# An FNet layer with a GEGLU block: wider loads of the DFT weights, another order of the first tiles, an earlier gate/up tile, down weights two steps ahead, and a plain tail

## The chip, the cores and the metric

The kernel runs on one core of a Trainium2 chip. Its engines work in parallel, each through its own queue in order: PE (TensorE, matmuls), PEld (its weight loads), DVE (VectorE), ACT (ScalarE), POOL (GpSimd) and SP (SyncE, which only issues DMAs here). The metric is the time on the device in microseconds, the median of several executions; lower is better. One further execution is recorded by the hardware profiler; its times of single instructions are used throughout.

## The reference

One sequence of 2048 tokens with 448 features, 1792 hidden features, all in float32.

```python
def mixing(x, seq_re, seq_im, hid_re, hid_im):
    a = jnp.einsum("bsd,ed->bse", x, hid_re)
    b = jnp.einsum("bsd,ed->bse", x, hid_im)
    return jnp.einsum("ts,bse->bte", seq_re, a) - jnp.einsum("ts,bse->bte", seq_im, b)

def geglu(x, w_gate, w_up, w_down):
    g = jnp.einsum("bsd,df->bsf", x, w_gate)
    u = jnp.einsum("bsd,df->bsf", x, w_up)
    return jnp.einsum("bsf,fd->bsd", gelu(g) * u, w_down)

h = x + mixing(layernorm(x), seq_re, seq_im, hid_re, hid_im)
out = h + geglu(layernorm(h), w_gate, w_up, w_down)
```

## The kernel before

Every float32 operand is split into two float16 parts, a high one (rounded, made on ACT by `hi_part`, line 100) and a low one (the remainder, made on DVE by `lo_part`, lines 104 and 106). A product is three float16 matmuls: high by high, high by low, low by high. Many products are done in Strassen form, which saves an eighth of the matmuls and pays with sums of blocks on DVE and POOL.

**Feature DFT.** x comes as 16 tiles of 128 tokens (`x_load`, line 307). Each is normalised, split, transposed by PE or by DMA (`x_turn`) and multiplied with the hidden DFT matrix: `feature_mm(i)`, slot "F", 22 matmuls of 448 columns in 11 steps of 2 (line 404). `feature_out` copies the result from PSUM (the tile `ab`) into the operands `b` of the next stage; for tiles of Strassen units it goes first into a float32 tile of the buffer ring "w" (two buffers).

**Sequence DFT.** 8 passes p over 256 output tokens each, with 8 units u of 256 input tokens in each pass: slot "U", `seq_mm(p, u)`, line 491. Units 5, 6 and 7 are Strassen units: 42 matmuls of 224 columns. The other five have 24 matmuls of 448. A unit's weights are loaded by SP into `wr` (`seq_load`, line 458, four buffers), summed on DVE if it is a Strassen unit (`seq_sums`, lines 463 to 465) and split into `ws` (`seq_split`, three buffers): high parts on ACT, low parts on DVE. `seq_out` (line 518 and the lines around it) ends a pass and adds the residual into `hx`. Pass 0 runs between the F slots; in passes 1 to 7, the FFN's layer norm and transposes for the passes that are done run beside it.

**Gate/up weights.** Between the units, 14 tiles of the gate and up weights are prepared (class `Weights`): loaded (line 538), summed on DVE (`gu_s`, lines 543 to 546), split on ACT and DVE into `gu_w` (also in the ring "w"; 4 sums and 4 splits on DVE for each tile), and stored by SP to DRAM (`w_dram`, line 571). The FFN loads them again as `gw` (line 928).

**Order.** The order of both DFTs is a plan: `plan(slot, rank, work)` puts a piece of work into a slot of the list `slots`; a slot's pieces are issued in the order of their ranks, and then its matmuls. What comes ahead of slot 3 is written out by hand.

**FFN.** 4 blocks of tokens by 14 tiles, in 56 steps t. `GateUp(t)` (line 848) has the matmuls into `pX`, `pY`, `pZ`, whose results are combined by DVE (line 858, `u`, `hh`, `c`), ACT and POOL. From step 14 on each step also has 21 down matmuls (line 791, `acc_d <- wd, dn_w`) for hidden tiles done earlier; `dn_w` is split on ACT and DVE. The down weights `wd` come in 7 tiles: `down_load(n)` (line 193), `down_sums(n)` on POOL (lines 198 to 201, `wd_s`), then splits in `down_prep(k)`, k = 0 to 13, two for each tile, on ACT and DVE.

**Tail.** After step 55, down products of the last hidden block remain for four output tiles of 128 tokens. One of the four is made plain (`last_mm`, line 1011: 84 matmuls of 224 columns) into the PSUM bank `last_tr`; two are made as a Strassen pair (`last_sums`, `last_split`, `last_pair_mm`: 147 matmuls, and sums `last_v`, `last_s`, `last_a` on DVE, POOL and ACT); the last is made plain into two banks, X and Y. `h_last` are the split hidden tiles, `hr` the tiles with the residual that go out (line 1023).

Of the kernel before, what the change touches and what calls it, by code (L numbers as in the profile page):

```python
# [8 lines left out]
F16 = mybir.dt.float16  # L9
# [4 lines left out]
P = 128  # L14
# [18 lines left out]
def kernel(  # L33
# [157 lines left out]
    def down_load(n):  # L191
        wd32[n] = fops.tile([P, 4, HD], F32, tag="xn" if n % 2 else "tt", name=f"wd32_{n}")
        nc.sync.dma_start(wd32[n].rearrange("p (k c) d -> p k (c d)", k=2), w_down[n])
# [100 lines left out]
    first = ExitStack()  # L294
    p1 = first.enter_context(tc.tile_pool(name="p1", bufs=1, side="right"))
# [85 lines left out]
    def wh_high(k):  # L381
        hi_part(wh_hi[:, k, :], wh_raw[k // 2][:, k % 2, :], D_SC)
# [12 lines left out]
    def feature_mm(i, parts=range(2), tag="B"):  # L395
        if 0 in parts:
            feat[i] = [ps_dft.tile([P, 512], F32, tag=tag, name=f"ab{i}_{r}") for r in range(2)]
        steps = [[], [(k, wh_lo, k) for k in range(4)]]
        for k in range(4):
            steps[0] += [(k, wh_hi, k)] + ([(4 + k, wh_hi, k)] if k < 3 else [])  # L400
        for part in parts:
            for n, (kx, w, kw) in enumerate(steps[part]):
                for r in range(2):
                    PE.matmul(  # L404
                        feat[i][r][:, :D],
                        xT[i][:, kx, :],
                        w[:, kw, r * D : (r + 1) * D],
                        start=part == 0 and n == 0,
                        stop=part == 1 and n == 3,
                    )  # L410
# [44 lines left out]
    def seq_load(p, u):  # L455
        wr[p, u] = dft.tile([P, 4, 2 * P], F32, tag="wr", bufs=4, name=f"wr{p}_{u}")
        for g in range(2):
            nc.sync.dma_start(wr[p, u][:, 2 - 2 * g : 4 - 2 * g, :], w_seq[p * N_UNIT + u, :, g::2, :])

    def seq_sums(p, u):  # L460
        r = wr[p, u]
        s = wsum[p, u] = dft.tile([P, 4, 2 * P], F32, tag="wsum", bufs=2, name=f"wsum{p}_{u}")
        V.tensor_add(s[:, 0:2], r[:, 0:1].to_broadcast([P, 2, 2 * P]), r[:, 1:3])  # L463
        V.tensor_add(s[:, 2], s[:, 0], r[:, 2])
# [14 lines left out]
    PRODUCTS = [(1, 0, 2, 0), (2, 2, 0, 1), (6, 1, 0, 0), (0, 6, 1, 1), (3, 3, 2, 1), (5, 5, 3, 0), (4, 4, 3, 1)]  # L479

    def seq_mm(p, u, first, last):
# [4 lines left out]
        for cc in range(2):  # L486
# [11 lines left out]
            else:  # L498
                for k, a0 in ((0, 2), (1, 0)):
# [165 lines left out]
    for k in range(1, 4):  # L665
        wh_load(k)
# [615 lines left out]
```

## Time and profile before

| | us |
|---|---|
| median of 3 runs | 746.25 (745.68 to 746.96) |
| profiled execution | 745.24 |
| its span in the profile | 743.4 |
| start, up to the first sequence unit | 0 to 31.39 |
| feature DFT and pass 0, to the end of pass 0 | 31.39 to 121.45 |
| passes 1 to 4 and a part of 5 | 121.45 to 284.81 |
| rest of the sequence DFT | 284.81 to 371.63 |
| FFN | 371.63 to 704.84 |
| tail | 704.84 to 743.4 |

A row of the timeline or of the chain reads: start, duration, engine, line of the kernel, operation, output <- inputs, partitions x elements and type, number of instructions; in brackets the engine's idle time ahead of it and what ended it. A row of the waits reads: who waited for whom, us in all, number, the longest.

In the page's division of the span into 40 slices, the busy share of PE in tenths, and its clock, are:

```profile
PE   7999999998989999999999989999999999999987
PEclk9999999999999999999999999999999999999999
```

### The profile page before, as it was taken

To read this page: it belongs to the slowest core of one execution; us is meant where nothing else is said; L and a number is where in the kernel's file an instruction comes from. 1 tells how busy PE (TensorE), PEld (TensorE's weight loads), DVE (VectorE), ACT (ScalarE), POOL (GpSimd) and SP (SyncE) were. 2 spreads that over 40 slices of the span, in tenths; PEclk is the share of its full clock that TensorE was granted. 3 is DMA by queue.
4 is the path that set the end of the run, shared out by engine and by line. 5 is a ranking of instruction groups with operands and counts; after the bars stand their busy time and mean duration, and the time that the engine had idled before them with its cause. 6 is when DMAs were issued, how large, how long until landed. Compare 5 with 4: busy or idle time off the path is not lost.

```text
span 743.4 us, 14813 instructions
## 1 busy us (share of the span) xinstructions
PE 716.3 (96%) x5779; PEld 559.1 (75%) x5779; DVE 599.0 (81%) x1165; ACT 329.4 (44%) x611; POOL 292.8 (39%) x316
## 2 busy tenths in 40 slices
PE   7999999998989999999999989999999999999987
PEld 4455557765656666677688868999999999999987
DVE  5677777898989899989447789788787877989795
ACT  5566553537363634444134444345444434444421
POOL 3033121010101020101047986577676766768460
PEclk9999999999999999999999999999999999999999
DMA  9154444788979789786167744656639475555311
GB/s 313 55 126 102 99 119 156 229 233 270 249 255 242 261 227 348 237 303 229 50 207 265 256 173 167 186 182 178 188 128 254 170 213 216 203 187 210 129 38 38
DMA packets 97927, 142.92 MB, mean 192 GB/s; under 512 B 42305, under 2 KB 81345, under 8 KB 97857
## 3 DMA queue, kind: packets, MB, share of 16 engines
q1 hardware_dynamic: 97856, 141.97, 60.9%
q8 instruction: 45, 0.74, 0.4%
q14 instruction: 26, 0.20, 0.1%
HBM read 112.46 MB, written 20.19 MB: 178 GB/s over the span
## 4 chain that ended last, share of the span: by engine, by line
PE 63%; DVE 21%; ACT 5%; DMA 4%; issue 3%; POOL 2%; SPq 1%; ACTq 0%; DVEq 0%; POOLq 0%
PE acc L491 18%; PE pY L848 12%; PE acc_d L791 11%; PE pX L848 8%; PE pZ L848 8%; PE ab L404 6%; DVE ws L106 5%; DVE gu_w L106 2%; DVE xs L104 1%; DVE wsum L463 1%; DMA x<-in_x_dram 1%; DMA gw<-w_dram 1%; DVE dn_w L104 1%; ACT ws L100 1%; DVE last_v L1032 1%
## 5 line engine op out<-in xcount | busy, mean ns | idle before, releaser
L491 PE MATMUL acc<-b,ws 128*128 128x448 f16 (+1 forms) x1968 | 282.7, 305 | 7.6 <-DVE ws L106 6.8
L491 PEld LDWEIGHTS <-ws 128*128 128x128 f16 x1968 | 188.8, 98 | 100.8 <-DVE ws L106 13.1
L848 PEld LDWEIGHTS <-gw 128*128 128x128 f16 x2067 | 202.3, 98 | 30.2 <-issue 6.5
L848 PE MATMUL pY<-hops,gw 128*128 128x256 f16 x901 | 123.2, 273 | 5.5 <-DVE u L858 5.2
L525 POOL TENSOR_TENSOR hx<-hx,e 128x448 f32<-128x448 f32 x16 | 25.2, 1594 | 253.3 <-DVE e L522 158.6
L791 PE MATMUL acc_d<-wd,dn_w 128*128 128x224 f16 x882 | 105.4, 259 | 0.0
L106 DVE SCALAR_TENSOR_TENSOR ws<-wr,ws 128x1024 f16<-128x1024 f32 (+1 forms) x64 | 76.7, 1199 | 15.0 <-ACT ws L100 14.8
L791 PEld LDWEIGHTS <-dn_w 128*128 128x128 f16 x882 | 85.2, 98 | 3.0
L100 ACT ACTIVATE ws<-wr 128x1024 f16<-128x1024 f32 (+1 forms) x64 | 61.6, 969 | 50.1 <-PE acc L491 25.2
L848 PE MATMUL pX<-hops,gw 128*128 128x256 f16 x583 | 81.3, 273 | 1.7 <-DMA gw<-w_dram 1.7
L848 PE MATMUL pZ<-hops,gw 128*128 128x256 f16 x583 | 79.7, 274 | 0.0
L858 DVE SCALAR_TENSOR_TENSOR u<-pY,u 128x256 f32<-128x256 f32 x112 | 47.0, 420 | 36.6 <-PE pY L848 18.2
L886 ACT ACTIVATE u<-pX 128x256 f32<-128x256 f32 x56 | 21.4, 382 | 90.4 <-PE pX L848 84.9
L404 PEld LDWEIGHTS <-xT 128*128 128x128 f16 x352 | 34.4, 99 | 34.3 <-issue 2.3
L915 POOL TENSOR_TENSOR hh<-hh,g 128x256 f32<-128x256 f32 x42 | 35.9, 855 | 57.8 <-DVE hh L858 57.8
L104 DVE TENSOR_TENSOR dn_w<-dn_s,dn_w 128x640 f16<-128x640 f32 x42 | 52.7, 1254 | 1.6 <-ACT dn_w L100 1.4
L899 ACT ACTIVATE g<-pX 128x256 f32<-128x256 f32 x56 | 21.3, 380 | 70.0 <-PE pX L848 66.5
L404 PE MATMUL ab<-wh_hi,xT 128*128 128x448 f16 x224 | 47.0, 360 | 1.1 <-DVE b L106 0.7
L100 ACT ACTIVATE ws<-wsum 128x1024 f16<-128x1024 f32 x24 | 25.3, 1054 | 50.9 <-DVE wsum L465 50.9
L941 POOL TENSOR_TENSOR dn_s<-hh 128x256 f32<-128x256 f32 x42 | 43.5, 1036 | 0.0
L924 POOL TENSOR_TENSOR hh<-hh,c 128x256 f32<-128x256 f32 x42 | 36.8, 877 | 16.3 <-ACT c L922 16.3
L942 POOL TENSOR_TENSOR dn_s<-hh 128x256 f32<-128x256 f32 x42 | 43.1, 1026 | 0.0
(134 smaller groups left out, 956.8 us busy)
## 6 DMA issues: line engine op xcount, KB each, us to landing
gw<-w_dram SPq DMA_DIRECT2D x53, 896.0 KB, 5.0
wr<-in_w_seq_dram SPq DMA_DIRECT2D x128, 256.0 KB, 4.9
w_dram<-gu_w SPq DMA_DIRECT2D x14, 896.0 KB, 4.8
gu_raw<-in_w_gu_dram SPq DMA_DIRECT2D x28, 384.0 KB, 4.7
wd<-in_w_down_dram SPq DMA_DIRECT2D x14, 448.0 KB, 4.9
hx<-in_x_dram SPq DMA_DIRECT2D x8, 448.0 KB, 5.8
h_dram<-hx SPq DMA_DIRECT2D x8, 448.0 KB, 5.2
hr<-h_dram SPq DMA_DIRECT2D x8, 448.0 KB, 5.4
```

The lines of the kernel that those rows point to most:

```text
L100: A.activation(dst, src, AF.Copy, scale=scale)
L104: V.tensor_sub(dst, src, hi)
L106: V.scalar_tensor_tensor(dst, src, scale, hi, op0=ALU.mult, op1=ALU.subtract)
L404: PE.matmul(feat[i][r][:, :D], xT[i][:, kx, :], w[:, kw, r * D : (r + 1) * D], start=part == 0 and n == 0, stop=part == 1 and n == 3,)
L491: PE.matmul(banks[k][:, cols], lhs, rhs, start=k not in begun, stop=stop, skip_group_check=True)
L791: PE.matmul(acc[k // 2][:, k % 2 * HD : (k % 2 + 1) * HD], a_of(la, a), b_of(lb, b), start=first and m == 0 and k % 2 == 0, stop=last and ...
L848: PE.matmul(ps, w[:, wl, wa + ws, :], ops[:, m + ms, :], start=first and n == 0, stop=last and n == len(terms) - 1, skip_group_check=True,)
L858: V.scalar_tensor_tensor(dst, ps, SC, other, op0=ALU.mult, op1=ALU.add)
L915: G.tensor_mul(c21, c21, self.g1)
L924: G.tensor_mul(c22, c22, self.c12)
L941: G.tensor_add(s[:, 0:2], t[:, 0:2], t[:, 2:4])
L942: G.tensor_sub(s[:, 2:4], t[:, 1:4:2], t[:, 0:4:2])
```

## The change

W's unit comes in one DMA, with rows of 4 KB for each partition, where two DMAs brought two blocks each. The blocks stand in another order, so the sums, the splits and the table of products name others; the split of a Strassen unit's own blocks falls into two pieces, of 256 and 512 elements, where it was one of 768.

```diff
     def seq_load(p, u):
...
-        for g in range(2):
-            nc.sync.dma_start(wr[p, u][:, 2 - 2 * g : 4 - 2 * g, :], w_seq[p * N_UNIT + u, :, g::2, :])
+        nc.sync.dma_start(wr[p, u], w_seq[p * N_UNIT + u])
...
-        V.tensor_add(s[:, 0:2], r[:, 0:1].to_broadcast([P, 2, 2 * P]), r[:, 1:3])
-        V.tensor_add(s[:, 2], s[:, 0], r[:, 2])
-        V.tensor_add(s[:, 3], s[:, 2], r[:, 3])
+        V.tensor_add(s[:, 0:2], r[:, 1:2].to_broadcast([P, 2, 2 * P]), r[:, 0:4:3])
+        V.tensor_add(s[:, 2], s[:, 1], r[:, 0])
+        V.tensor_add(s[:, 3], s[:, 2], r[:, 2])
...
-        parts = [(slice(0, 3), r[:, 1:4]), (slice(3, 7), wsum.pop((p, u)))] if is_s(u) else [(slice(0, 4), r)]
+        parts = [(slice(0, 1), r[:, 0:1]), (slice(1, 3), r[:, 2:4]), (slice(3, 7), wsum.pop((p, u)))] if is_s(u) else [(slice(0, 4), r)]
```

The first of the 14 gate/up tiles is prepared inside the feature DFT, and the other 13 are spread over the passes; a tile's load and its store each come one slot later. `p2`, the pool of their raw tiles, is there from the start. x is loaded, normalised and transposed two slots earlier than before.

```diff
-            plan(n - 8, 8, lambda u=i // 2: x_load(u))
+                plan(n - 10, 8, lambda u=i // 2: x_load(u))
...
-        plan(n - 2, 3, lambda p=p, u=u: seq_split(p, u))
+        plan(n - 2 if g else -3, 3, lambda p=p, u=u: seq_split(p, u))
...
-            plan(g, 9, lambda p=p, u=u: seq_load(p, u))
+            plan((-6, -5, 1, 2)[g], 9, lambda p=p, u=u: seq_load(p, u))
...
-    n0 = p1_end + 4
+    pairs = [where["F", 2 * u] for u in ORDER if is_s(u)]
+    early_f = [s + 4 for s in pairs[1:2]]
+    n0 = p1_end + 3
...
-    at_f = [n0 + k * (len(slots) - 3 - n0) // NF for k in range(NF)]
-    plan(n0 - 3, 9, lambda: gu.update({order[0]: Weights(order[0])}))
+    late_f = NF - len(early_f)
+    at_f = early_f + [n0 + k * (len(slots) - 5 - n0) // late_f for k in range(late_f)]
+    plan(0, 9, lambda: gu.update({order[0]: Weights(order[0])}))
...
-            plan(n + 1, 9, lambda f=order[k + 1]: gu.update({f: Weights(f)}))
-        plan(n + 2, 7, lambda f=f: gu[f].split(False), lambda f=f: gu[f].store())
+            plan(n + 2, 9, lambda f=order[k + 1]: gu.update({f: Weights(f)}))
+        plan(n + 2, 7, lambda f=f: gu[f].split(False))
+        plan(n + 3, 10, lambda f=f: gu[f].store())
```

In the feature DFT, DVE's queue has these rows before, around the Strassen unit 6 of pass 0 (`ws_6`) and the feature tiles 14 and 15 (`b_14`, `b_15`; the numbers at the ends of names are the program's own):

```order
L463 TENSOR_TENSOR wsum_6_962<-wr_6_410 128x512
L464 TENSOR_TENSOR wsum_6_962<-wsum_6_962,wr_6_410 128x256
L465 TENSOR_TENSOR wsum_6_962<-wsum_6_962,wr_6_410 128x256
L106 SCALAR_TENSOR_TENSOR ws_6_990<-wr_6_410,ws_6_990 128x768
L106 SCALAR_TENSOR_TENSOR ws_6_990<-wsum_6_962,ws_6_990 128x1024
L104 TENSOR_TENSOR xs_996<-x_780,xs_996 128x64
L104 TENSOR_TENSOR xs_996<-x_780,xs_996 128x384
```

And these rows now, at the same place of the same queue:

```order
L466 TENSOR_TENSOR wsum_6_985<-wr_6_446 128x512
L467 TENSOR_TENSOR wsum_6_985<-wsum_6_985,wr_6_446 128x256
L468 TENSOR_TENSOR wsum_6_985<-wsum_6_985,wr_6_446 128x256
L106 SCALAR_TENSOR_TENSOR gu_w_989<-gu_raw_419,gu_w_989 128x512
L106 SCALAR_TENSOR_TENSOR gu_w_989<-gu_raw_419,gu_w_989 128x256
L106 SCALAR_TENSOR_TENSOR ws_6_1019<-wr_6_446,ws_6_1019 128x256
L106 SCALAR_TENSOR_TENSOR ws_6_1019<-wr_6_446,ws_6_1019 128x512
L106 SCALAR_TENSOR_TENSOR ws_6_1019<-wsum_6_985,ws_6_1019 128x1024
L106 SCALAR_TENSOR_TENSOR gu_w_989<-gu_s_945,gu_w_989 128x512 x2
L104 TENSOR_TENSOR b_1093<-b_14_1059,b_1093 128x1568
```

The four splits of the early gate/up tile stand between the sums and behind the splits of unit 6, the 768 is a 256 and a 512, and the split of the last x tiles (`xs`) stands further ahead. On ACT the copy into `b_15` now waits for the DMA that stores `gu_w_989`, since both use the same buffer of the ring.

Of the start, written out by hand, this is the core. The loads of x for tiles 0 and 1 stand ahead of the four loads of the hidden matrix, `feature_mm` is cut in parts of its 11 steps, and the high part of the matrix's last block is made on GpSimd.

```diff
-    wh_load(0)
     x_load(0, (slice(1, 2),))
-    for k in range(1, 4):
+    for k in range(4):
         wh_load(k)
     x_load(1)
+    x_load(ORDER[2])
...
+    wh_high(3, G)
...
-    wh_high(3)
...
-    feature_mm(0, (0,))
+    feature_mm(0, range(6))
+    x_stats(2)
     x_turn_pe(1, 0, 4)
     x_turn_pe(1, 4, 7)
+    feature_mm(0, range(6, 7))
```

The down weights are prepared two steps earlier, and their first load and sums lie within the sequence DFT.

```diff
+    plan(len(slots) - 14, 9, lambda: down_load(0))
+    plan(len(slots) - 8, 9, lambda: down_sums(0))
...
-    down_load(0)
     down_load(1)
...
-            if t == 2:
-                down_sums(0)
-            if t > 2:
-                down_prep(t - 3)
+            if t > 0:
+                down_prep(t - 1)
...
-        if t - 3 <= 2 * NC:
-            down_prep(t - 3)
+        if t == 2 * NC:
+            down_prep(t - 1)
```

DVE's queue in step 15 of the FFN (the number behind `u_` is the step) has these rows before:

```order
L858 SCALAR_TENSOR_TENSOR u_15_5102<-pY_5087,u_15_5100 128x256
L106 SCALAR_TENSOR_TENSOR wd<-wd_6_4925,wd 128x448
L104 TENSOR_TENSOR dn_w_5120<-hh_4106,dn_w_5120 128x256
L104 TENSOR_TENSOR dn_w_5120<-dn_s_5050,dn_w_5120 128x640
L858 SCALAR_TENSOR_TENSOR u_15_5146<-pY_5087,u_15_5100 128x256
L858 SCALAR_TENSOR_TENSOR hh_4999<-pZ_5108,u_15_5146 128x256
```

And these now:

```order
L882 SCALAR_TENSOR_TENSOR u_15_5097<-pY_5082,u_15_5095 128x256
L104 TENSOR_TENSOR dn_w_5112<-hh_4101,dn_w_5112 128x256
L104 TENSOR_TENSOR dn_w_5112<-dn_s_5045,dn_w_5112 128x640
L882 SCALAR_TENSOR_TENSOR u_15_5138<-pY_5082,u_15_5095 128x256
L882 SCALAR_TENSOR_TENSOR hh_4998<-pZ_5103,u_15_5138 128x256
```

The split of `wd` is gone from there, and likewise the one of 128x1120 in step 16; the last two now stand in steps 13 and 14, where those of the tile before stood.

The tail makes all four tiles plain. `last_sums`, `last_split` and `last_pair_mm` go.

```diff
-    last_mm(1, 0, banks[:1])
-    for n in range(2):
+    for n, (j, g) in enumerate(((0, 0), (0, 1), (1, 0))):
+        last_mm(j, g, banks[n : n + 1])
         do(N_GU + 1 + n, 3)
...
-        last_pair_mm(n)
...
+        last_out(j, g, banks[n], 0, 2)
+    last_mm(1, 1, banks[3:])
+    for c in range(2):
+        last_out(1, 1, banks[3 + c], c, 1)
```

More of the change, by code (lines that the diff above doesn't have):

```diff
@@ L393, with feature_mm @@
     feat = {}
-    def feature_mm(i, parts=range(2), tag="B"):
-        if 0 in parts:
+    def feature_mm(i, part=range(11), tag="B"):
+        if 0 in part:
             feat[i] = [ps_dft.tile([P, 512], F32, tag=tag, name=f"ab{i}_{r}") for r in range(2)]
[L398 to L410, printed above, removed]
+        steps = [(k, wh_hi, n) for k, n in ((0, 0), (1, 1), (4, 0), (5, 1), (2, 2), (6, 2), (3, 3))]
+        steps += [(k, wh_lo, k) for k in range(4)]
+        for n in part:
+            kx, w, kw = steps[n]
+            for r in range(2):
+                PE.matmul(
+                    feat[i][r][:, :D],
+                    xT[i][:, kx, :],
+                    w[:, kw, r * D : (r + 1) * D],
+                    start=n == 0,
+                    stop=n == 10,
+                )
     HD = D // 2
```

111 lines of the change are left out of this document (43 added, 68 removed).

## The prediction

> **What bounds the kernel now.** I read the page first, then the span cut into its stages, then in each stage the waits of the engine that sets its pace. The page's own lines:
>
> ```profile
> span 743.4 us, 14813 instructions
> PE 716.3 (96%) x5779; PEld 559.1 (75%) x5779; DVE 599.0 (81%) x1165; ACT 329.4 (44%) x611; POOL 292.8 (39%) x316
> PE 63%; DVE 21%; ACT 5%; DMA 4%; issue 3%; POOL 2%; SPq 1%; ACTq 0%; DVEq 0%; POOLq 0%
> ```
>
> TensorE (PE) is busy for 716 of 743 us, so a change that leaves the matmuls alone can win only what PE waits, and what a lowered clock costs after a wait. The chain of work that ended last nevertheless runs through VectorE (DVE) for 21% of the span. The stages tell where (columns: start and end, length, busy us of PE, PEld, DVE, ACT, POOL, each with its count, then clock, DMA share, GB/s):
>
> ```profile
> 8.72:31.39 22.67, 20.21 (x112) 10.02 (x111) 12.85 (x35) 12.67 (x23) 4.32 (x2) 0.93 0.51 170
> 31.39:121.45 90.06, 89.21 (x533) 51.64 (x532) 66.16 (x127) 50.54 (x78) 20.16 (x18) 1.00 0.47 119
> 121.45:284.81 163.36, 155.96 (x1099) 104.51 (x1097) 148.94 (x284) 77.61 (x118) 16.27 (x10) 1.00 0.82 243
> 284.81:371.63 86.82, 86.82 (x604) 58.52 (x605) 71.00 (x119) 34.66 (x50) 6.69 (x4) 1.00 0.67 226
> 371.63:461.46 89.83, 83.11 (x745) 73.17 (x744) 65.09 (x126) 37.86 (x82) 63.37 (x67) 0.98 0.61 213
> 704.84:743.40 38.56, 32.68 (x317) 30.70 (x315) 29.15 (x57) 7.45 (x12) 14.51 (x17) 0.96 0.10 37
> ```
>
> PE waits 2.5 us in the start (first row), 0.9 in the feature DFT, 7.4 in the first half of the sequence DFT, nothing in its second half, 6.7 in the first 90 us of the FFN, and some 3 before the last store in the tail; the 243 us of FFN between the last two rows are full. These are the only places where this change can find time, and the terms below take them one by one.
>
> **The tail: -3.4.** The last seven units of a Strassen pair (147 matmuls) and two plain tiles (168) become four plain tiles of 84, which is 21 matmuls more. Rows of the timeline, of the windows and of the chain:
>
> ```profile
> 704.84 0.26 PE L1011 MATMUL last_tr<-wd,h_last 128*128 128x224 f16 x1
> 718.08 2.49 PE L791 MATMUL acc_d<-wd,last_a 128*128 128x224 f16 x13 [2.14 <-DVE last_a L104]
> 718.08:722.00 3.92, 3.92 (x24) 3.25 (x25) 3.85 (x9) 0.74 (x1) 1.40 (x3) 0.56 0.49 176
> 732.43 4.03 PE last_X L1011 x42
> 736.45 4.04 PE last_Y L1011 x42
> 707.38 1.09 DVE L104 TENSOR_TENSOR h_last<-hq,h_last 128x512 f16<-128x512 f32 x1 [0.26 <-ACT h_last L100]
> ```
>
> 42 plain matmuls take 4.03 us, 96 ns each. From the first one at 704.84, 336 x 0.096 = 32.2 us end at 737.1, where the last one ends now at 736.45 + 4.04 = 740.5: -3.4. The present tail is slower with fewer matmuls because DVE makes the Strassen sums: PE waits 2.14 us for them once, and in the 3.92 us after that wait the clock is 0.56, which costs 3.92 x 0.44 = 1.7. The new order needs only the h tiles; the last of them is ready at 707.38 + 1.09 = 708.5, and the first plain tile, which takes them in order, wants it with its last 6 of 84 matmuls, at 704.84 + 78 x 0.096 = 712.3. What follows the last matmul (an addition and a store of the same size) stays. Bounds: -1.7, if the clock is low there all the same, and -3.4.
>
> By the Trainium skill, TensorE: Matmul & The Clock Gate, Part 1, the clock falls only after an idle window of some 3.4 us, so a wait of 2.14 us should not lower it, the 1.7 us would come from elsewhere and might stay, and the term would be -1.7. The trace speaks against that: in both places where PE waits over 2 us (here, and 2.29 us at 441.89 below) the clock stands at half right behind the wait.
>
> **Down's weights: -2.1.** Down's weights are split on ACT and DVE in 14 parts, two for each of 7 tiles, with sums on POOL. Before, step t of the FFN makes part t - 3, through step 16; now part t - 1, through step 14. PE has its first down matmul of steps 14, 15, 16 and 17 at:
>
> ```profile
> 436.51 0.93 PE L791 MATMUL acc_d<-wd,dn_w 128*128 128x224 f16 x8
> 446.82 0.93 PE L791 MATMUL acc_d<-wd,dn_w 128*128 128x224 f16 x8
> 454.03 0.93 PE L791 MATMUL acc_d<-wd,dn_w 128*128 128x224 f16 x8
> 461.46 0.93 PE L791 MATMUL acc_d<-wd,dn_w 128*128 128x224 f16 x8
> 467.73 0.93 PE L791 MATMUL acc_d<-wd,dn_w 128*128 128x224 f16 x8
> 446.92 1.25 DVE L106 SCALAR_TENSOR_TENSOR wd<-wd,wd 128x448 f16<-128x448 f32 x1
> 453.99 1.61 DVE L106 SCALAR_TENSOR_TENSOR wd<-wd_s,wd 128x1120 f16<-128x1120 f32 x1
> 441.89 1.23 PE L848 MATMUL pY<-hops,gw 128*128 128x256 f16 x5 [2.29 <-DVE u L858]
> ```
>
> The full step is 467.73 - 461.46 = 6.27. Steps 15 and 16 take 7.21 and 7.43, 0.94 and 1.16 more, and in each a weight split (1.25 and 1.61) stands on DVE ahead of the dn_w and u that PE waits for. Without them nothing is late there: step 17 has the same other work in 6.27. So -2.1. Step 14 takes 10.31, 4.04 more: the wait of 2.29 and a halved clock behind it. There the order of DVE around c_13, wd, dn_w and u_14 is the same afterwards, only with the other weight tile, so I let it stay; that it goes too is a rival. Steps 1 to 12 get their weights earlier; DVE has 25 us free in that window, so nothing is charged. Bounds: 0 and -2.1.
>
> **The fourth gate/up load: -1.3.** One of the two down loads that are issued at the start of the FFN moves 14 slots ahead.
>
> ```profile
> 384.78 0.83 PE L848 MATMUL pX<-hops,gw 128*128 128x256 f16 x6 [1.30 <-DMA gw<-w_dram]
> wd<-in_w_down_dram SPq DMA_DIRECT2D x14, 448.0 KB, 4.9
> gw<-w_dram SPq DMA_DIRECT2D x53, 896.0 KB, 5.0
> ```
>
> PE waits 1.30 for gate/up tile 3, whose load is issued right behind the two of down, 448 KB each. It comes at 384.78 and is wanted at 383.48. The two have together the bytes of one gw, which takes 5.0 in the median; without one of them the gw has half of that less ahead of it, up to 2.5. More than 1.30 is of no use: -1.3, bounds 0 and -1.3.
>
> **The start: -1.0.** Tiles 0 and 1 of x are now loaded ahead of the weights, the first matmuls follow the weights' order of arrival, and one weight conversion goes to GpSimd.
>
> ```profile
> 8.72 4.36 PE L404 MATMUL ab<-wh_hi,xT 128*128 128x448 f16 x14
> 27.23 2.81 PE L404 MATMUL ab<-wh_hi,xT 128*128 128x448 f16 x14
> 11.85 2.44 POOL L390 TENSOR_SCALAR wh_raw<-wh_raw 64x896 f32<-64x896 f32 x1 [9.60 <-ACT wh_hi L100]
> 12.61 0.71 DVE L104 TENSOR_TENSOR xs<-x,xs 128x64 f16<-128x64 f32 x2
> ```
>
> Fourteen matmuls take 4.36 us at the start and 2.81 later, so 1.55 are lost on late weights there, and the stage's PE waits are 2.46 in all: the most to be won is some 3. The same four tiles and transposes must still run before the first sequence unit at 31.39, and the loads ahead of them still come one behind another; placing each step behind what it needs gives me some 0.9 earlier. I take -1.0. Bounds: -3, and +2.4 if the conversion on GpSimd (its nearest row is 2.44) stands on the path as a whole.
>
> By the Trainium skill, SBUF — State Buffer, Who interferes with whom, a GpSimd instruction that reads SBUF locks out a DVE one with two SBUF inputs until it ends, so the new conversion would hold DVE's xs for up to 2.4, and the term would be +1.4. The last two rows show the two side by side, 0.71 unhindered, so I charge none of it.
>
> **The sequence DFT: -1.5.** It is DVE that paces the stage from 121 to 285: 148.94 of 163.36 us busy, and the largest waits of PE there are for it.
>
> ```profile
> PE acc L491 <- DVE ws L106: 6.7, 15, 1.1
> 201.98 1.02 DVE L106 SCALAR_TENSOR_TENSOR gu_w<-gu_raw,gu_w 128x512 f16<-128x512 f32 x2
> 207.52 1.29 DVE L106 SCALAR_TENSOR_TENSOR gu_w<-gu_s,gu_w 128x512 f16<-128x512 f32 x2
> 202.91 0.95 DVE L106 SCALAR_TENSOR_TENSOR ws<-wr,ws 128x768 f16<-128x768 f32 x1
> 201.17 0.43 DVE L464 TENSOR_TENSOR wsum<-wsum,wr 128x256 f32<-128x256 f32 x1
> ```
>
> With one gate/up tile made in the feature DFT and the rest spread wider, the four passes of that stretch hold 64 DVE instructions for gate/up tiles instead of 70. At 0.51 to 0.65 each that is 6 x 0.58 = -3.5. Against it, a Strassen unit's split of 768 becomes one of 256 and one of 512: 0.43 + 0.58 - 0.95 = about +0.1 on DVE, in 12 units +1.2. That leaves -2.3, of which I take two thirds, since some of PE's waits follow from an order of instructions and not from the sum: -1.5, bounds +1.2 and -3.5. W's single load per unit for two saves SP an issue each, but neither PE nor DVE waits for W's loads there: 0.
>
> **The early gate/up tile: 0.** Its 8 DVE instructions (8 x 0.55 = 4.4 us) lie in the feature DFT, where DVE has 24 us free, PE waits 0.9. It brings one new wait: the copy of feature tile 15 out of PSUM goes into the buffer of this tile, so ACT holds it until the tile's store has landed.
>
> ```profile
> 100.18 2.81 PE L404 MATMUL ab<-wh_hi,xT 128*128 128x448 f16 x14
> 92.00 0.98 ACT L100 ACTIVATE b<-ab 128x448 f32<-128x448 f32 x2 [1.93 <-PE ab L404]
> w_dram<-gu_w SPq DMA_DIRECT2D x14, 896.0 KB, 4.8
> 85.72 1.23 DVE L106 SCALAR_TENSOR_TENSOR ws<-wsum,ws 128x1024 f16<-128x1024 f32 x1 [0.25 <-ACT ws L100]
> ```
>
> The tile's last DVE pair (1.29) stands behind the ws at 85.72, so it ends about 88.3; the store lands 4.8 later, about 93, or 95 with queueing, where the copy now starts at 92.0. Behind it on ACT stand the halves of b for tiles 14 and 15 and of the next W unit; PE wants the two banks again only for a feature tile at 100.18. So ACT waits 1 to 3 us and PE none.
>
> **Sum.** -3.4 - 2.1 - 1.3 - 1.0 - 1.5 = -9.3. The profiled execution took 745.24 (span 743.4), so its like would take 735.9; the median shown, 746.25, is 1.0 above it, and I forecast **737.0**.
>
> **The rivals.**
> *Nothing from start and sequence.* The orders there only move waits about. The three other terms give -6.8, 739.5; with the upper bound of 1.2 for the splits and half of that for the start, 741.5. For it: in the sequence stage ACT waits on DVE and DVE on ACT. Against it: the busy share of 91%.
> *More than I count.* The 4.0 of step 14 goes too, since three POOL sums of down's weights that stand in step 14 now come two steps earlier: 733.0. For it: the stall is a near miss of crowded engines. Against: the same order around u_14.
> *The clock in the tail is low anyway* (the rule above): -1.7 less, 738.7.
> *Slower: the copy of tile 15 is held long.* The price is one for one from the point where the store lands later than about 100: ACT then stands, PE gets no bank and the next W unit no high half. To end slower than before by more than the measurement can tell it would have to land beyond 111, 18 us later than I have it. SP waits for DVE ahead of these stores up to 9.3 (13 times, by the row below), and a store lands 4.8 after its issue: the worst wait alone would bring it to 102, so it takes that twice over.
>
> ```profile
> SPq L571 <- DVE gu_w L106: 47.9, 13, 9.3
> ```
>
> That the change does not do what it says I exclude: the order of instructions shows each part.
>
> **How the numbers follow.** Forecast 0.55 (own range 734.5 to 739), nothing from start and sequence 0.22 (739 to 742.5), more 0.14 (730.5 to 734.5), clock 0.04, slower 0.05. A difference of 0.2%, 1.5 us, is about what a measurement of this kernel can tell from none. The range 732.5 to 742.0 leaves out the slower case, a third of the case of more and a small end of the other, in all under 0.2. Faster 0.92, same 0.03, slower 0.05.
>
> **What would show it.** In the new profile: no wait of PE behind the first of the last four tiles and 32.2 us of matmuls there; steps 15 and 16 of the FFN at 6.27; no wait for the fourth gate/up tile; the first sequence unit before 31; PE's waits in the first half of the sequence DFT near 6; the copy of tile 15 held 1 to 3 us by a DMA, with no wait of PE in the 10 us after it. It would be wrong if PE's waits for ws grow, if step 14 changes, or if the copy is held beyond 100.

## The result, and the profile after

The changed kernel takes 742.17 us in the median of 11 runs (740.11 to 745.5), the kernel before 746.56 in 11 runs beside it (745.68 to 747.17): a ratio of 0.9948 with a 95% interval of 0.9933 to 0.9963. It is faster by 4.4 us, where 9.3 were forecast, and lies just above the range. It also scatters more: 5.4 us between its runs, against 1.5 before; but beside the experiments below the kernel before scattered by 2.5 to 4.0.

The profiled execution took 745.5 us, the slowest of its eleven. The page's first lines:

```profile
span 743.7 us, 14694 instructions
PE 718.5 (97%) x5800; PEld 562.3 (76%) x5800; DVE 582.2 (78%) x1150; ACT 322.3 (43%) x624; POOL 289.1 (39%) x310
```

The kernel after, cut where PE begins a new stage (first feature matmul, first sequence unit, end of the last feature tile, first gate/up matmul, first plain tail matmul; columns as in the prediction):

```profile
9.14:34.80 25.66, 21.99 (x112) 10.98 (x110) 19.00 (x47) 12.73 (x24) 6.79 (x3) 0.87 0.47 159
34.80:108.92 74.12, 72.42 (x422) 41.01 (x421) 51.24 (x110) 40.56 (x68) 20.45 (x18) 1.00 0.48 124
108.92:376.45 267.53, 259.85 (x1812) 173.60 (x1811) 236.97 (x437) 121.58 (x198) 26.04 (x17) 1.00 0.72 229
376.45:708.27 331.82, 325.93 (x3067) 298.71 (x3066) 264.77 (x531) 141.99 (x326) 227.41 (x255) 0.99 0.60 195
708.27:743.70 35.43, 32.37 (x338) 32.11 (x336) 6.29 (x12) 1.21 (x3) 6.84 (x10) 1.00 0.11 40
```

And the kernel before, cut at the same events, where the prediction's rows have other cuts:

```profile
31.39:104.51 73.12, 72.27 (x422) 40.93 (x421) 55.00 (x112) 43.90 (x70) 20.16 (x18) 1.00 0.45 107
104.51:371.63 267.12, 259.72 (x1812) 173.73 (x1811) 231.09 (x416) 118.92 (x176) 22.96 (x14) 1.00 0.76 233
371.63:704.84 333.21, 326.00 (x3068) 298.69 (x3067) 266.82 (x531) 141.95 (x326) 229.31 (x258) 0.99 0.60 196
```

The lengths of these stretches say where the time went in these two executions: the start +3.4 (34.80 against 31.39), the feature DFT +1.0, the sequence DFT +0.4, the FFN -1.4, and the tail's matmuls -3.3 (they end at 740.63, 32.36 after 708.27; before at 740.47, 35.63 after 704.84). Together that is +0.2, as the two profiled times say (745.5 against 745.24): the gain that the medians show is not in this profile. The tail gains as forecast, the FFN less than half of it, and the front loses.

**The start.** The timeline of the kernel after, where PE waits, and the windows behind it:

```profile
16.30 1.87 POOL L396 TENSOR_TENSOR wh_lo<-wh_raw,wh_hi 64x896 f16<-64x896 f32 x1
16.36 2.38 DVE L104 TENSOR_TENSOR xs<-x,xs 128x64 f16<-128x64 f32 x2
18.32 0.23 PE L370 MATMUL xT_ps<-ident,xs 128*128 128x128 f16 x1 [1.48 <-DVE xs L104]
19.40 5.63 PE L408 MATMUL ab<-wh_hi,xT 128*128 128x448 f16 x20
...
21.00:23.00 2.00, 2.00 (x7) 0.89 (x6) 1.56 (x7) 0.30 (x1) 0.00 (x0) 0.50 0.00 0
```

DVE's pair of `xs` takes 2.38 us, 0.69 elsewhere. It begins 0.06 us behind GpSimd's low part of the last block, and ends 0.57 us after it. PE waits 1.48 for it and soon runs at half clock (last row): 20 matmuls take 5.63 us, where 14 take 2.81 at full clock, which makes 4.0.

**The feature DFT.** PE now waits here once more than before for DVE's low halves of `b`. They come late by way of ACT: its `sd_x` waits 3.76 for statistics of x, which DVE makes behind `xs` and `wsum`; the high half of `b` stands behind `sd_x` on ACT, and the low half needs the high one.

```profile
65.25 0.29 ACT L121 ACTIVATE sd_x<-mv_x,eps_t 128x2 f32<-128x2 f32 x1 [3.76 <-DVE mv_x L316]
66.01 1.16 DVE L106 SCALAR_TENSOR_TENSOR b<-ab,b 128x448 f16<-128x448 f32 x2 [0.79 <-ACT b L100]
66.69 0.35 PE L408 MATMUL ab<-wh_hi,xT 128*128 128x448 f16 x1 [0.90 <-DVE b L106]
```

**The early gate/up tile** held ACT for longer than the forecast's 1 to 3 us, and came within 0.3 us of holding PE:

```profile
96.98 0.33 SPq L574 DMA_DIRECT2D w_dram<-gu_w  x1
103.33 0.98 ACT L100 ACTIVATE b<-ab 128x448 f32<-128x448 f32 x2 [7.60 <-DMA w_dram<-gu_w]
104.59 2.81 PE L408 MATMUL ab<-wh_hi,xT 128*128 128x448 f16 x14
```

The copies end at 104.31; PE wants the banks at 104.59.

**The FFN.** First down matmuls of steps 15, 16 and 17, PE's waits in step 14 (2.29) and for gate/up tile 3, the fourth (1.10), and the clock behind the wait of step 14:

```profile
389.39 0.83 PE L872 MATMUL pX<-hops,gw 128*128 128x256 f16 x6 [1.10 <-DMA gw<-w_dram]
447.08 1.23 PE L872 MATMUL pY<-hops,gw 128*128 128x256 f16 x5 [2.29 <-DVE u L882]
452.08 0.93 PE L815 MATMUL acc_d<-wd,dn_w 128*128 128x224 f16 x8
458.35 0.93 PE L815 MATMUL acc_d<-wd,dn_w 128*128 128x224 f16 x8
464.62 0.93 PE L815 MATMUL acc_d<-wd,dn_w 128*128 128x224 f16 x8
447.08:449.00 1.92, 1.92 (x10) 1.32 (x10) 1.92 (x4) 0.20 (x1) 1.60 (x3) 0.51 0.00 0
```

Steps 15 and 16 take 6.27 each, as forecast. Step 14 keeps its 2.29. The load of tile 3 is waited for 1.10 us, hardly less than before.

**The tail.** In the chain of work that ended last, four plain tiles stand one behind another:

```profile
708.44 8.05 PE last_tr L1035 x84
716.49 8.05 PE last_X L1035 x84
724.54 8.05 PE last_Z L1035 x84
732.59 4.03 PE last_Y L1035 x42
736.61 4.04 PE last_a L1035 x42
```

### The profile page after: what moved, and what is told of

Same layout as the page of the kernel before. It is cut to its first block, busy times and chain, and to the rows that moved or that the text cites. A ratio compares the mean times of both kernels' runs of the same rounds, so it can differ in the third digit from the quotient of the medians.

```text
span 743.7 us, 14694 instructions
## 1 busy us (share of the span) xinstructions
PE 718.5 (97%) x5800; PEld 562.3 (76%) x5800; DVE 582.2 (78%) x1150; ACT 322.3 (43%) x624; POOL 289.1 (39%) x310
## 4 chain that ended last, share of the span: by engine, by line
PE 56%; DVE 4%; DMA 3%; POOL 1%; ACT 1%; issue 1%; DVEq 0%; POOLq 0%; ACTq 0%
PE acc L494 14%; PE pY L872 12%; PE acc_d L815 11%; PE pX L872 8%; PE pZ L872 7%; DMA gw<-w_dram 3%; PE last_Z L1035 1%; PE last_X L1035 1%; PE last_tr L1035 1%; DVE dn_w L104 1%; DVE ws L106 1%; PE last_a L1035 1%; PE last_Y L1035 1%; DVE xs L104 0%; ACT ws L100 0%
## 5 line engine op out<-in xcount | busy, mean ns | idle before, releaser
L106 DVE SCALAR_TENSOR_TENSOR ws<-wr,ws 128x1024 f16<-128x1024 f32 (+2 forms) x88 | 79.3, 925 | 13.7 <-ACT ws L100 13.2
L100 ACT ACTIVATE ws<-wr 128x1024 f16<-128x1024 f32 (+2 forms) x88 | 63.4, 755 | 42.2 <-issue 31.4
L408 PE MATMUL ab<-wh_hi,xT 128*128 128x448 f16 x224 | 48.6, 370 | 1.8 <-DVE b L106 1.7
```

The costliest lines, as they stand in the source:

```text
L100: A.activation(dst, src, AF.Copy, scale=scale)
L106: V.scalar_tensor_tensor(dst, src, scale, hi, op0=ALU.mult, op1=ALU.subtract)
L408: PE.matmul(feat[i][r][:, :D], xT[i][:, kx, :], w[:, kw, r * D : (r + 1) * D], start=n == 0, stop=n == 10,)
```

## The experiments

Each kernel was timed in five rounds beside the kernel before on the same chip (the ratio is to that one, with its 95% interval), and profiled once. The stretches are PE's, cut as above.

| kernel | median us | ratio | start | feature | sequence | FFN | tail |
|---|---|---|---|---|---|---|---|
| before | 746.56 | | 31.39 | 73.12 | 267.12 | 333.21 | 35.63 |
| changed | 742.17 | 0.9948 (0.9933 to 0.9963) | 34.80 | 74.12 | 267.53 | 331.82 | 32.36 |
| 1 changed, again | 742.64 | 0.9937 (0.9920 to 0.9953) | 34.22 | 74.13 | 267.60 | 330.18 | 32.36 |
| 2 changed, old start | 738.52 | 0.9888 (0.9873 to 0.9902) | 32.26 | 73.12 | 266.96 | 329.00 | 32.35 |
| 3 changed, no early tile | 741.94 | 0.9939 (0.9927 to 0.9951) | 32.74 | 74.13 | 266.99 | 330.34 | 32.37 |
| 4 before, plain tail | 742.97 | 0.9950 (0.9938 to 0.9962) | 31.61 | 73.10 | 268.54 | 333.50 | 32.37 |
| 5 changed, low part on DVE | 741.61 | 0.9929 (0.9914 to 0.9943) | 31.85 | 74.13 | 267.66 | 330.96 | 32.36 |
| 6 changed, x later | 740.60 | 0.9921 (0.9906 to 0.9936) | 34.33 | 71.78 | 267.20 | 331.21 | 32.37 |
| 7 changed, down parts doubled | 743.14 | 0.9950 (0.9936 to 0.9964) | 31.84 | 74.12 | 267.88 | 332.10 | 32.37 |
| 8 before, W loads | 747.21 | 1.0010 (0.9998 to 1.0022) | 31.89 | 73.10 | 267.61 | 333.02 | 35.64 |
| 9 as 2, down parts from step 0 | 738.97 | 0.9902 (0.9889 to 0.9916) | 31.50 | 73.11 | 267.31 | 329.20 | 32.36 |
| 10 as 2, no early tile | 740.14 | 0.9915 (0.9893 to 0.9938) | 31.53 | 73.12 | 269.21 | 332.34 | 32.36 |
| 11 as 2, additions on DVE | 735.09 | 0.9849 (0.9836 to 0.9861) | 32.14 | 73.11 | 262.88 | 329.36 | 32.37 |
| 12 changed, 5 and 6 | 738.42 | 0.9895 (0.9880 to 0.9911) | 32.53 | 71.78 | 267.39 | 329.69 | 32.36 |
| 13 as 11, down parts from step 0 | 735.20 | 0.9851 (0.9836 to 0.9865) | 32.01 | 73.12 | 263.04 | 330.73 | 32.37 |
| 14 before, additions on DVE | 742.26 | 0.9949 (0.9934 to 0.9963) | 33.18 | 73.11 | 264.52 | 332.51 | 35.64 |
| 15 as 2, again | 739.74 | 0.9914 (0.9900 to 0.9928) | 31.90 | 73.11 | 267.00 | 328.87 | 32.36 |
| 16 as 10, again | 740.74 | 0.9929 (0.9910 to 0.9947) | 31.89 | 73.10 | 268.84 | 331.42 | 32.36 |
| 17 as 12, additions on DVE | 734.66 | 0.9855 (0.9830 to 0.9881) | 31.35 | 71.78 | 262.85 | 331.62 | 32.36 |

Between executions of one kernel the start differs by up to 0.6, the FFN by up to 1.6 and the sequence DFT by up to 0.4 (number 1 against the changed one, 2 against 15, 10 against 16); the feature DFT and the tail repeat to 0.02.

**1 and 2: is the start the loss?** Number 2 has the hand-written start of before, its order of a tile's eleven steps, x two slots later and the first loads of W in their old slots.

```diff
-    x_load(0, (slice(1, 2),))
-    for k in range(4):
-        wh_load(k)
+    wh_load(0)
+    x_load(0, (slice(1, 2),))
+    for k in range(1, 4):
+        wh_load(k)
...
-                plan(n - 10, 8, lambda u=i // 2: x_load(u))
+            plan(n - 8, 8, lambda u=i // 2: x_load(u))
```

> The changed kernel once more, for a second profile. In the first one the first sequence unit begins at 34.80 us (before: 31.39) and the last feature tile ends at 108.75 (before: 104.50), and its time, 745.5, is the slowest of its eleven runs. If the start's loss of 3.4 us is the rule, the first unit begins again near 34.8 and the median is near 742; if that profile caught an unusual stretch of low clock, the first unit begins at 31 to 33 and the profiled time is 740 to 742.

> The changed kernel with the start of the kernel before: its hand-written order, its order of the eleven steps of a feature tile, x two slots later, the first loads of W in its slots. Theory S (the new start loses what the rest gains): 3 us less than the changed kernel, near 739, first sequence unit at 31.4. Rival (the early gate/up tile and the sequence stage lose it): same as the changed kernel or up to 1 us slower.

The loss repeats (34.22, with the same 2.37 for the two `xs`), and the old start ends it: 738.52, 3.7 to 4.1 less than the changed kernel. Run again as number 15, it gave 739.74, 2.4 to 2.9 less.

**3, 10, 15 and 16: what is the early tile worth?**

```diff
-    early_f = [s + 4 for s in pairs[1:2]]
+    early_f = []
```

> The changed kernel with all fourteen gate/up tiles spread over the passes, none in the feature DFT. If the copy of feature tile 15, held 7.6 us by the early tile's store, costs PE: 1 to 3 us less than the changed kernel, and the last feature tile ends 0.8 to 1 us earlier. If the early tile is worth what was forecast (six DVE instructions fewer in four passes): 1 to 2 us more.

> The changed kernel with the start of before (738.5), and all fourteen gate/up tiles spread over the passes. If the early tile is worth the 1.5 us that was forecast for the sequence stage: 740. If it is worth nothing: 738.0 to 739.0, and the PE's stretch from the last feature tile to the FFN stays at 267.

> The changed kernel with the start of before once more (738.5), beside the next run on one chip. 738 to 739; PE's stretch from the last feature tile to the FFN 267 us.

> The same without the early gate/up tile, once more (740.1 in a wide interval, 736.6 to 743.4). If the early tile is worth the forecast 1.5 us: 1 to 2 us above the run beside it; if nothing: within 0.5 us of it.

With the old start the tile shortens the sequence stretch by 1.8 in the pair run side by side (267.00 against 268.84) and the median by 1.0, though the runs of the two overlap (738.08 to 741.29 and 738.87 to 742.94). With the new start it was worth nothing (3 against the changed kernel). So it gains some 1 to 2 us or less, and the long wait of ACT costs PE nothing: the feature stretch is the same with and without it.

**4: the tail by itself.** The edit is the change's last piece, put into the kernel before.

```diff
-        last_pair_mm(n)
...
+    for n, (j, g) in enumerate(((0, 0), (0, 1), (1, 0))):
+        last_mm(j, g, banks[n : n + 1])
```

> The kernel before with only the plain tail. By the first profile of the changed kernel, whose tail takes 32.2 us where the one before takes 35.65: 3.4 us less than before, 743. Rival (the earlier sums of the Strassen pair ran beside other work, and part of the gain depends on the rest): 2 us less or nothing.

742.97 against 746.45: -3.5, as expected, and PE's stretch is 32.37 for 35.63.

**5, 6 and 12: which part of the start?**

```diff
-    wh_low(3, G)
...
     wh_low(2)
+    wh_low(3)
```

> The changed kernel, with the low part of the hidden matrix's last block made on DVE behind the other three, not on GpSimd (where 13.76 to 18.17 us were two instructions, and beside them DVE's two xs took 2.38 us for 0.69, PE waited 1.48 for them, and the clock then stood at half from 20.7 to 24.3). If that collision is the start's loss: first sequence unit 1.5 to 3 us earlier than 34.5, and 1.5 to 3 us less than the changed kernel (742.4), that is 739.5 to 741. If the order of the loads and steps as such is to blame: within 0.7 of it, since DVE has 1.1 us more to do.

```diff
-                plan(n - 10, 8, lambda u=i // 2: x_load(u))
+                plan(n - 8, 8, lambda u=i // 2: x_load(u))
...
-                    plan(n - 5, 5, lambda i=c: x_norm(i), lambda i=c: x_lo(i))
-                plan(n - 4, 2, lambda i=c: x_turn(i))
+                    plan(n - 3, 5, lambda i=c: x_norm(i), lambda i=c: x_lo(i))
+                plan(n - (2 if k > 2 else 4), 2, lambda i=c: x_turn(i))
```

> The changed kernel, with x from the third pair of tiles on two slots later, as before; the start as changed. If the feature DFT's extra microsecond (PE from the first sequence unit to the last feature tile: 74.1 against 73.1 before; a wait of 0.90 and 0.18 for b on DVE at 66.7) comes from x's work standing ahead of b on DVE: 73.1 here and 1 us less than the changed kernel. If it comes from the start: 74.1 and the same time.

> The changed kernel with its own order of loads and steps at the start, but the low part of the last block on DVE (alone: 741.6) and x two slots later from the third pair on (alone: 740.6). If these two are the start's whole loss: 738.5 to 739, as with the start of before. If the order of the loads and steps has its own part, by first matmuls that wait 1.65 to 1.87 for xT and a later wait of 2 us at 26: 739.5 to 740.5.

Number 5 brings the first sequence unit to 31.85, but lowers the median by only 0.6 to 1.0; number 6 takes 2.35 from the feature DFT (1 was expected) and 1.6 to 2.0 from the median. Both together give 738.42, what the old start gives, so the order of the loads and steps neither loses nor gains anything that the runs can tell. By their medians the two repairs add to 2.1 to 3.1 and together give 3.8 to 4.2; why they should be worth more together is open, at medians of four and five runs.

When the collision comes, the order of two starts decides. Numbers 1, 3, 6 and 7 have the same instructions there as the changed kernel. In number 1 GpSimd is first by 0.05 us, as in the changed kernel by 0.06, and DVE is held. In numbers 3, 6 and 7 DVE is first, as here in number 7:

```profile
15.11 0.69 DVE L104 TENSOR_TENSOR xs<-x,xs 128x64 f16<-128x64 f32 x2
15.23 2.31 POOL L396 TENSOR_TENSOR wh_lo<-wh_raw,wh_hi 64x896 f16<-64x896 f32 x1
```

DVE takes its 0.69, and GpSimd's instruction 2.31 instead of 1.87: 0.44 more, of the 0.57 that DVE still had to run.

What the collision costs, the stretches from the begin of this `xs` to the first sequence unit show, in the changed kernel, in number 7 and in number 6:

```profile
16.36:34.80 18.44, 15.59 (x82) 7.93 (x81) 14.11 (x35) 8.46 (x16) 1.82 (x1) 0.91 0.24 66
15.11:31.84 16.73, 13.53 (x80) 7.24 (x78) 13.30 (x35) 8.24 (x16) 2.35 (x2) 1.00 0.32 95
15.92:34.33 18.41, 15.64 (x83) 8.07 (x82) 14.95 (x39) 9.10 (x18) 2.34 (x2) 0.91 0.25 67
26.05 0.33 PE L370 MATMUL xT_ps<-ident,xs 128*128 128x128 f16 x3 [2.08 <-ACT xT L371]
26.22 4.12 PE L408 MATMUL ab<-wh_lo,xT 128*128 128x448 f16 x12
```

With DVE held it is 18.44 (in number 1 too), without 16.73 (in number 3 too). The difference of 1.7 is the halved clock alone: 20 matmuls take 5.63 for 3.95, while the wait of 1.48 is made up by a later wait for `xT`, 0.68 in the changed kernel and 2.33 in number 7. Number 6 has the same 1.7 without DVE being held: there the clock falls behind the later wait (last two rows; the 12 matmuls take 2.43 in number 7). The clock fell in this stretch in both profiles in which DVE was held, and in one of the six of the new start in which it was not (numbers 3, 5, 6, 7, 12 and 17). So the hold seems to bring the low clock more often, but eight profiles don't show that it is the cause.

**7, 9 and 13: the wait that stayed in step 14.**

```diff
-            if t > 0:
-                down_prep(t - 1)
+            if 0 < t < 11:
+                down_prep(t - 1)
+            if t in (11, 12):
+                down_prep(2 * t - 12)
+                down_prep(2 * t - 11)
```

> The changed kernel, with the last parts of down's weights made two by two in steps 11 and 12, so that steps 13 and 14 have none. If the split of 128x1120 ahead of dn_w and u on DVE is what PE waits 2.29 us for in step 14 (and 1.3 to 1.5 in step 13): both waits go, 3 to 5 us less than the changed kernel. If dn_w's own chain through POOL is: the wait of step 14 stays above 1.5 us, and at most 1 us is gained.

```diff
-                down_prep(t - 1)
+            for k in [t] if t < 3 else [3, 4] if t == 3 else [t + 1] if t < 13 else []:
+                down_prep(k)
```

> The changed kernel with the start of before (738.5), and down's weights one step earlier still (part t in steps 0 to 2, two parts in step 3, part t + 1 through step 12), so that the last parts stand apart from each other and none is in step 13 or 14. The run that put two parts each into steps 11 and 12 lost the wait of 2.29 in step 14 and got one of 3.87 in step 12: weight splits ahead of dn_w on DVE move the wait to where they stand. By that theory the 2.29 of step 14 goes and step 13's 1.3 to 1.5 stays: 2.3 to 4 us less (with a halved clock behind it or not), 734.5 to 736.5. Rival (the same DVE work is late somewhere in steps 0 to 4): within 1 us of 738.5.

```diff
-            if t > 0:
-                down_prep(t - 1)
+            down_prep(t)
```

> The changed kernel with the start of before and the additions on DVE (735.1), and down's weights one more step earlier, part t in step t from 0 to 13, never two in a step. The run with two parts in step 3 lost the waits of step 14 and got one of 2.07 in step 3. If that was the double part alone: the 2.29 of step 14 goes, step 13's wait stays, 732 to 733.5. If a part in steps 0 to 2 costs as much: within 0.7 of 735.1.

PE's waits in the timelines of 7, 9 and 13, one after another:

```profile
434.67 1.23 PE L872 MATMUL pY<-hops,gw 128*128 128x256 f16 x5 [3.87 <-DVE u L882]
```

```profile
398.14 0.71 PE L853 MATMUL pX<-hops,gw 128*128 128x256 f16 x5 [2.07 <-ACT u L891]
```

```profile
429.23 0.71 PE L853 MATMUL pY<-hops,gw 128*128 128x256 f16 x5 [2.77 <-DVE u L863]
439.41 0.71 PE L853 MATMUL pY<-hops,gw 128*128 128x256 f16 x5 [1.09 <-DVE u L863]
```

Where no split stands in step 14, the wait of 2.29 goes or shrinks (to 1.09 in number 13), and another comes or grows. Summed over these steps PE waits 3.6 in the changed kernel (2.29, and 1.29 in step 13) and 3.8 in number 2, against 3.9 in number 7, 3.6 in 9 (2.07 and 1.51) and 3.9 in 13. None of the three gained, and the gains of some 2 to 5 us that were expected if the splits were the cause didn't come. Moving a part within the first 14 steps moved the wait.

**8: W's loads by themselves.** The edit is the change's first piece (one load, new order of blocks, three pieces of the split), put into the kernel before.

```diff
-        for g in range(2):
-            nc.sync.dma_start(wr[p, u][:, 2 - 2 * g : 4 - 2 * g, :], w_seq[p * N_UNIT + u, :, g::2, :])
+        nc.sync.dma_start(wr[p, u], w_seq[p * N_UNIT + u])
```

> The kernel before with W's units in one load of 4 KB rows and the split of 256 and 512 that this needs, nothing else. By the forecast's count (0.1 us of DVE for each of 21 Strassen splits in a stage that DVE paces, nothing from the DMAs): 1 to 2 us slower than before. Rival (the larger rows come earlier and free SP): 1 us faster. Neither: within 0.7 us of before.

747.21 against 746.64, an interval from 0.9998 to 1.0022: no difference that the runs can tell, and the 1.2 that was charged lies within it.

**11, 14 and 17: what paces the sequence DFT?**

```diff
-            G.tensor_add(h[:, g], h[:, g], e[:, 2 * g : 2 * g + 2].rearrange("p o d -> p (o d)"))
+            V.tensor_add(h[:, g], h[:, g], e[:, 2 * g : 2 * g + 2].rearrange("p o d -> p (o d)"))
```

> The changed kernel with the start of before (738.5), and the two residual additions at the end of each pass on DVE instead of GpSimd. Beside GpSimd's 3.2 us DVE's ws took 2.13 for 1.23 and wsum 1.62 for 0.69, in each pass: 1.8 us. If DVE's time in these passes sets the pace, 0.7 us less of it (1.8 less 1.1 for the additions) in each of four to seven passes: 735 to 737. If an order of instructions sets it: within 0.7 us of 738.5.

> The kernel before with only the two additions at a pass's end on DVE. If the sequence stage of before is paced by DVE being held beside GpSimd's additions (1.8 us in each pass): 3 to 4 us less than before, 742.5 to 743.5, as in the changed kernel with the old start. If the pace was another one before: less than 1 us.

> The changed kernel with its start, the low part of the last block on DVE, x two slots later (these two alone: 738.4) and the residual additions on DVE (worth 3.4 to 3.9 in the two runs so far). If the gains are of separate stages they add: 734.5 to 735, and PE's stretches are 71.8 in the feature DFT and 263 in the sequence DFT. Rival (the shorter feature DFT only brings DVE's pace forward): the sequence stretch grows by what the feature DFT saves, 735.5 to 736.5.

The end of a pass in number 2, with the additions on GpSimd:

```profile
197.17 3.20 POOL L525 TENSOR_TENSOR hx<-hx,e 128x448 f32<-128x448 f32 x2 [34.51 <-DVE e L522]
197.25 2.13 DVE L106 SCALAR_TENSOR_TENSOR ws<-wr,ws 128x1024 f16<-128x1024 f32 x1
199.31 1.62 DVE L463 TENSOR_TENSOR wsum<-wr 128x512 f32<-128x512 f32 x1
```

And in number 11, with them on DVE:

```profile
195.64 1.15 DVE L525 TENSOR_TENSOR hx<-hx,e 128x448 f32<-128x448 f32 x2
196.70 1.22 DVE L106 SCALAR_TENSOR_TENSOR ws<-wr,ws 128x1024 f16<-128x1024 f32 x1
197.84 0.69 DVE L463 TENSOR_TENSOR wsum<-wr 128x512 f32<-128x512 f32 x1
```

DVE gets 1.15 us more to do, and has 1.84 less (2.13 + 1.62 - 1.22 - 0.69); a hold of 1.7 us or more stands at the end of all seven passes of number 2. The sequence stretch falls by 4.1 and the median by 3.4, to 735.09. In the kernel before the same edit gives 742.26 for 746.15, -3.9 (its profiled stretch falls by 2.6). So DVE, held beside GpSimd, paces a part of this stage in both kernels; that the additions also end some 2 us earlier was not tested apart. Number 17 has all repairs, 734.66: its feature and sequence stretches are as expected, but its FFN in that profile is 331.62, and it can't be told from number 11. Both beat the changed kernel by 7 us and the one before by 11.

## Why the prediction was wrong

**The tail (-3.4): right in size, with one wrong reason.** 32.36 for 35.63 in the profile, -3.5 alone on the chip, and the sum of 336 matmuls stands. But the forecast put 1.7 us of the old tail down to the clock of 0.56 behind the wait of 2.14. Number 8 has the old tail with the same wait and a full clock behind it, and takes 35.64 all the same, since PE then waits for DVE's sums once more:

```profile
718.85 1.42 PE L790 MATMUL acc_d<-wd,last_a 128*128 128x224 f16 x13 [2.14 <-DVE last_a L104]
721.98 1.42 PE L790 MATMUL acc_d<-wd,last_a 128*128 128x224 f16 x13 [0.94 <-DVE last_a L104]
718.85:722.77 3.92, 2.98 (x30) 2.73 (x31) 3.85 (x9) 0.74 (x1) 1.40 (x3) 1.00 0.48 173
```

DVE's sums paced the old tail; the low clock there cost nothing, and the bound of -1.7 has no ground in these runs.

**Down's weights (-2.1): right.** Steps 15 and 16 are at 6.27, and step 14 kept its wait, as assumed. Steps 14 to 16 together take 22.92 in the profile of the changed kernel and 21.44 in number 2, where the clock stays full behind the same wait. With the old steps they take 24.95 at half clock (before) and 25.00 at full clock (number 8), where PE waits longer for DVE in step 15 instead. The FFN as a whole takes 328.87 to 332.34 in the twelve profiles that have it as changed, and 332.51 to 333.50 in the four that have it as before; the 1.4 that the first profile gains is among the smallest.

**The fourth gate/up load (-1.3): mis-sized.** PE waits 1.10 for it, 1.30 before. The down load ahead of it was not the only reason that it was late: in other profiles with the same FFN the wait for tile 3 is 0.23 and 0.36 (numbers 2 and 15) and missing (number 1), and in number 14, which has the old order, it is missing too. Somewhere from 0.2 to 1.3 is gained, and the forecast took the upper end.

**The start (-1.0): the step that failed.** The gain did not come, and a loss came that was charged with nothing.

The forecast read 14 matmuls in 4.36 for 2.81 as 1.55 lost on late weights. The window of these matmuls in the kernel before shows the clock instead (0.66; 4.36 x 0.34 = 1.5), with PE busy throughout and so no wait for weights in it:

```profile
8.72:13.08 4.36, 4.36 (x19) 1.77 (x18) 2.33 (x7) 3.33 (x6) 1.23 (x1) 0.66 1.05 381
```

In the profiles whose clock is full from the first feature matmul to the first sequence unit, that unit begins at 31.50 to 31.90 with the old start (numbers 4, 8, 9, 10 and 15) and at 31.35 and 31.84 with the new one (17 and 7): nothing is gained that can be told.

The loss: "The last two rows show the two side by side, 0.71 unhindered, so I charge none of it." The rows showed a GpSimd instruction with one tensor input (TENSOR_SCALAR) beside DVE's `xs` of another tile. The one that follows it on GpSimd has two (TENSOR_TENSOR), and before only its end touched an `xs` (14.38 to 16.25, and 16.14). The conversion that is new on GpSimd pushes it to 16.30, beside the `xs` at 16.36, and it held DVE. The first unit is late by 3.4 and 2.8 in two profiles, and by 0.45 in number 7, where DVE was first. Of that, 1.7 is the halved clock behind the hold; the rest lies ahead of this `xs`, which begins anywhere between 14.59 and 16.36 in the profiles of the new start, and no run isolates why. By the medians, taking GpSimd's instruction away is worth 0.6 to 1.0 (number 5). By the Trainium skill, SBUF — State Buffer, Who interferes with whom, a DVE instruction with two SBUF inputs contends with a GpSimd one that reads SBUF, and whichever issues first holds the other for its whole length; the trace agrees for the two-input form on GpSimd, in both orders (2.38 and 2.31). For the one-input form it agrees only where DVE is first: `xs` takes 0.71 beside the 2.44 already running, but GpSimd's `wh_hi` takes 2.75 in number 3, begun 0.25 behind an `xs`, and 2.45 in the changed kernel.

The bound of +2.4 for this term allowed for GpSimd's conversion on the path; the +3.4 of the one profile lies beyond it, and the value chosen left it out. The scatter is not shown to come from it: number 10, which has the old start, scatters by 6.9.

**The feature DFT (0): left out.** The prediction worked out the early tile there, and left out that x's own work comes two slots earlier. The order on DVE and ACT is changed by it, and the low half of b, which frees PE's banks, came later: +1.0 against before, and 2.35 against the same start without the shift (number 6). Every moved step was to be charged; this one was not.

**The sequence DFT (-1.5): the pace was named, but not what makes it.** DVE does set a part of it. But the gain was counted from the number of instructions at their usual durations; the 1.8 us of each pass in which DVE is held by GpSimd's additions were not seen, and moving these away is worth 3.9 in the kernel before (number 14). The charge for the split was too low as well: its two pieces take 0.46 and 0.73 in the mean of this stretch, against 0.99 for the one of 768, so 0.2 more in each unit, not 0.1. And DVE is busy for longer in this stretch than before, not shorter (236.97 with 437 instructions, 231.09 with 416), because the splits come in more pieces and work on `b` and `ws` slid past the last feature tile. What the count forecast is partly there (the early tile 1 to 1.8 in the pair of 15 and 16; the split at most 1.2 in 8), yet the whole shows +0.4 in one profile. Kernels 4 and 8 have 268.54 and 267.61 where before has 267.12, so a profile can't settle a microsecond here.

**The early tile (0): right for PE, wrong for the wait.** ACT was held 7.6 us, since its store was issued at 96.98, where the forecast's 88.3 with the later front (4.4, by the feature tile at 104.59 for 100.18) makes 92.7, and landed 6.4 later for 4.8. The slower rival was 0.3 us from the point at which it begins to cost, though far from making the kernel slower.

With the old start the rest of the change gives 738.52 and 739.74; the forecast without its start term is 738.0. So of the 5.2 by which the median missed, 1.0 is the start's gain that didn't come, 2.4 to 3.7 the loss in the start and the feature DFT, and 0.5 to 1.7 all the rest. The measured time lies in the range of the rival "nothing from start and sequence", but that rival named no loss; it reached so far only by its upper bounds (739.5 + 1.2 + 0.6, which is 741.3 and not 741.5).

## What to carry to other kernels

Before moving work on VectorE, or work on GpSimd ahead of it, list what GpSimd runs at that time in the new order, not in the old one: here a hold of 1.7 us appeared where none was, and which of the two engines waits hung on some 0.1 us. Before charging a low clock, look whether PE sets the pace there, and in more than one profile. Three times a split was moved out of step 14 here, and each time PE's wait came back at another step; whether less work, or work on another engine, removes it was not tried. Charge every shifted line of a plan, also those that look like mere lead time.

## What the runs showed of the hardware

The halved clock behind a wait is not a property of the wait. After the same 2.29 us in step 14 the clock is 0.51 in the changed kernel (447.08 to 449.00, above) and full in number 12:

```profile
441.88 0.71 PE L872 MATMUL pY<-hops,gw 128*128 128x256 f16 x5 [2.29 <-DVE u L882]
441.88:443.80 1.92, 1.92 (x18) 1.75 (x18) 1.92 (x5) 0.19 (x1) 1.61 (x3) 1.00 0.00 0
```

Ten matmuls against 18 in the same 1.92 us. The prediction read the low clock of one profile as a rule; the Trainium skill, TensorE: Matmul & The Clock Gate, Part 1, calls the window that watches for activity free-running, and so variable from run to run, which these profiles bear out, though they also show that a wait of 2.3 us can be followed by half clock. What the half clock costs depends on what paces the stage: 1.7 us in the start and 1.5 in steps 14 to 16 of the changed kernel (22.92 for 21.44), nothing in these steps of the kernel before or in its tail.
